# Down-projection weights fetched as whole tiles, row stores and reloads lagged, and weight preparation respaced in an adaLN transformer block on Trainium2

## The chip, the core and the metric

The kernel runs on one core of a Trainium2 chip, in one launch. A core has a matrix engine (TensorE, "PE" in the profile, with its weight loads shown apart as "PEld"), a vector engine (VectorE, "DVE"), a scalar engine (ScalarE, "ACT"), a general engine (GpSimd, "POOL"), and a sync engine (SyncE, "SP"), which in this kernel does one thing: it issues every DMA, in the order in which it is given them. The metric is the device time of one execution in microseconds (us), lower is better.

## The reference

One transformer block with conditioning, S = 2048 rows of D = 512:

```python
mod = (silu(c) @ w_mod)                    # six rows of 512: sa, ca, ga, sb, cb, gb
h = layernorm(x) * (1 + ca) + sa
q = h @ wq                                 # 32 heads of 128
k, v = last 512 rows of the cache          # 8 kv heads, each for 4 q heads
x = x + ga * (softmax(q k^T * 128**-0.5) v) @ wo
h = layernorm(x) * (1 + cb) + sb
x = x + gb * (gelu(h @ w_gate) * (h @ w_up)) @ w_down      # width 1792
```

## The kernel before

**Arithmetic.** Every operand of a large product is held as a pair of fp16 tiles, high and low part, and every product of two such pairs is three matmuls: high by high, high by low, low by high (`mm3`, lines 85, 86 and 87). Projections and the feed-forward part save products by a seven-product scheme for 2x2 blocks: sums and differences of the weight blocks are formed once, stored in DRAM (`KEPT`, tile name kept) and fetched again as "sets" of tiles w, w0 to w2 and x3.

**Attention** is 512 slots, numbered t (T = 512); a slot is 128 rows of one head against 512 keys. PE makes the scores of slot t in one of two PSUM banks named ps (`scores`). DVE takes their maximum (nm, L939). ACT takes the exponential (ee, L948), which frees the bank for slot t+2. Two slots later ACT writes the high part of the probabilities (p, L962), one slot after that DVE writes the low part (L967), and SP transposes them by DMA (pt, L971) for the product with v (po). Rows of wo (py), the query projections (qa, qb, qc) and the accumulation into acc (L888) lie between. In attention the order on every engine is written out by hand: each piece of side work is put at a slot.

**Weight preparation.** The feed-forward weights must be scaled, split and stored before the feed-forward part. That is side work of slots 286 to 511, in seven rounds of 30 slots, n = 0 to 6: gate set `prep_set(2n)`, up set `prep_set(2n+1)`, and two blocks of w_down (`prep_wd`). A `prep_set` that begins at slot b loads two tiles rw (2 buffers, so each load needs a buffer that POOL has finished with), has ACT take the sum of squares of each (`sumsq`, writes junk, L216) at slots b+1 and b+2, gets its scale fsc from DVE (L293) at b+7, and has POOL scale, combine and split them (L160, L1360, L156, L157) from b+7 to b+12. The rw buffers come free at b+11 and b+12. A load is put at the slot three ahead of its use, or one after its buffer comes free if that is later, though never after the slot of its use:

```python
        go = pos[0] - ahead
        free = released[kind].pop(0) + LDGAP
        pending[kind].append((max(min(max(go, free), pos[0]), 0), max(free + 3, pos[0] - 9), load))
```

**Feed-forward part.** 28 rows q of seven products each. The first pass (q below 14) does the first half of the rows of x and multiplies its results with w_down as it goes (`y_tasks`, whole tiles wo). The second pass (q from 14) does the other half, and its down-projection is a list of products: `down` for pairs of hidden blocks in three groups, 14 products for each, then eight of `down_last`. Each `down` product fetches what it needs of w_down just before: two halves of 128 KB of two stored tiles (`fetch_w`, called by `prefetch` four to six products ahead). At the change of passes the eight finished row tiles acc are stored to the output (`f_final`), and the same buffers take the partial rows y of the other half (`load_facc`), up to two reloads pending until row q = 16. In the feed-forward part only SP's queue has its order written by hand.

Of the kernel before, what the change touches and what calls it, by code (L numbers as in the profile page):

```python
# [17 lines left out]
P = 128  # L18
# [44 lines left out]
def block_kernel(ctx: ExitStack, tc: tile.TileContext, x, kT, v, wq, wo, wg, wu, wd, cT, wc, wm, out):  # L63
# [192 lines left out]
    def w_spread(pr, m, w=None):  # L256
        w, u, t, r = w or w_first(m), little("lu", 1, 2), little("lt", 1, 2), little("lr", 1, 2)
        pool_ts(u, w, col("kmax", pr // 2), col("ma"))
        nc.gpsimd.tensor_tensor(t, u, half_, op=ALU.pow)
        pool_ts(t, t, TOP15, 1.0, ALU.min)  # L260

        def inv():
            nc.vector.reciprocal(r, t)

        def last():
            pool_ts(col("qsc", pr), t, 2.0 ** -26)
            pool_ts(r, r, u)
            pool_ts(col("ksc", pr), r, col("kinv", pr // 2))

        if now[0] >= 0:  # L270
            then(lambda: (nc.vector.reciprocal(col("wsc", pr), w), inv(), last()), 3 if pr > 1 else 2)
        return inv, last

    def y_scale(qd):
        pool_ts(col("ysc", qd), col("ysc", qd), col("vmax", qd), 1.0 / TOP15)
# [748 lines left out]
    def begin():  # L1024
        now[0] = -1
        for i in range(QT):
            na[i][0]()
            na[i][1]()
        na[2][2]()
        na[3][2]()  # L1030
        na[0][2]()
        na[1][2]()
        na[2][3]()
        na[3][3]()
        for key in ("B", "C", "Y", "T2", "T1"):
# [12 lines left out]
        m = {}  # L1048
        pair_stat(0, m, 0)
        pair_stat(0, m, 1)  # L1050
        k0[1]()
        ts(cols[:, 1, :], cols[:, 1, :], 1.0, None, ALU.add)
        ts(cols[:, 0, :], mps[:, 0:KT], 1.0, None, ALU.mult)
        pst = {}

        def mid():
            o0[0][0]()
            pst["w"] = sums(m["m"], 2)
            o0[1][0]()
# [12 lines left out]
        for n in range(1, KT):  # L1072
            o0[n][1](False)
            o0[n][3]()
            if n == 1:
                o0[0][2](nc.gpsimd)
            if n == 2:
                inv_k()
                inv_t()
                last()  # L1080
        warm(4)
        low_w(0)
        o0[1][2]()
        o0[2][2](nc.gpsimd)
        low_k = k0[3](True)
        o0[3][2]()
        low_k()
        nb[0][0]()
        nb[0][1]()
        high_w(1)  # L1090
        q_first(warm)
        v0[1]()
        run(("d", 0))
        low_w(1)
# [297 lines left out]
    def prep_wd(n, b):  # L1392
        m, st = {}, {}
        outs = [staged() for _ in range(4)]
        l, r = slice(0, 256), slice(256, 512)

        def load(k):
            st[k] = raw("raw")
            dma(st[k], wd[(2 * n + k) * P:(2 * n + k + 1) * P, :])

        def stat(k):
            if not m:
                m["m"] = little("lm", 4, dtype=BF16)
            sumsq(m["m"][:, k:k + 1], st[k])

        def spread():
            d_spread(n, m["m"])

        def scaled(k):
            nc.gpsimd.tensor_tensor(st[k], st[k], rows[5], op=ALU.mult)  # L1410
            times(st[k], col("dsc", n))

        def minus(o, a, b):
            nc.gpsimd.tensor_tensor(st[o[0]][:, o[1]], st[a[0]][:, a[1]], st[b[0]][:, b[1]], op=ALU.subtract)

# [24 lines left out]
        if n < NP - 1:  # L1440
            sched(b + 11, (more, [s2, nop]), b + 13)
            sched(b + 12, (outs[2][1], [lambda: halves(outs[2][0]["t"], st[2]), keep_it(2)]), b + 15)
            sched(b + 13, (outs[3][1], [lambda: halves(outs[3][0]["t"], st[0]), keep_it(3)]), b + 16)

    at(T // 2 + 34, lambda: mod_row(5))
    for n in range(NP):
        b = T // 2 + 30 + 30 * n
        prep_set(2 * n, b)
        prep_set(2 * n + 1, b + 14)
        prep_wd(n, b + 23)  # L1450
    for k in range(2):
        at(T - 1 + 2 * k, lambda k=k: WO.update({("f", 0, k): fetch(("wd", 0, k), get_wo())}))
    for q, ps_ in ((0, (T - 18, T - 17, T - 16, T - 15)), (1, (T - 8, T - 7, T - 3, T)), (2, (T + 2, T + 3, T + 4, T + 5))):
# [135 lines left out]
                post()  # L1589
                run(("d", now[0] + 1))  # L1590

    load_later, ready, queue = [], [], []
    facc, done_to = {}, [0]
    SPOT = {1: (1, 0), 2: (0, 0), 3: (0, 1), 4: (3, 0), 5: (2, 0), 6: (2, 1), 7: (3, 1)}
    INTO = {1: (1, 0), 2: (1, 0), 6: (1, 1), 7: (0, 1), 4: (0, 0), 5: (0, 1), 3: (1, 1)}
    YORDER = (1, 2, 6, 7, 4, 5, 3)
# [12 lines left out]
    FACC = [(1, 0, 0), (1, 0, 1), (0, 0, 1), (0, 0, 0), (1, 1, 0), (1, 1, 1), (0, 1, 1), (0, 1, 0)]  # L1609

    def f_final(ti):
        dma(rows_of(out, ti), acc[ti])
        load_later.append(FACC.pop(0))

    def down(ns, u, k, st):
        box = {}

        def fetch_w():
            box["w"] = get_wo().rearrange("p a (n c) -> p n a c", n=2)
            j, side = SPOT[k]  # L1620
            for i, n in enumerate(ns):
                dma(box["w"][:, i], KEPT["wd", n % NP, j][:, :, side * 256:side * 256 + 256])

        def go():
            key = "a" if k in (1, 6, 7, 4) else "b" if k == 2 else "c"
# [2 lines left out]
            for r in range(2):  # L1628
                ps = st[key][:, r * 256:r * 256 + 256]
                sl = slice((2 * u + r) * P, (2 * u + r + 1) * P)  # L1630
                for i, n in enumerate(ns):
                    t, w = A[n][k], box["w"][:, i]
                    mm3(ps, t[:, 0, sl], t[:, 1, sl], w[:, 0, :], w[:, 1, :], r + i == 0 and k in (1, 2, 5), r == 1 and i == len(ns) - 1 and k in (2, 4, 3), True)
            q, h = INTO[k]
            flat = facc[q, u, h].rearrange("p r c -> p (r c)")
            by = col("dmx", ns[0] % NP // 2)
            nc.vector.scalar_tensor_tensor(flat, st[key], by, flat, op0=ALU.mult, op1=ALU.add)

        return fetch_w, go

    plain = {}

    def down_last(u, q, h, first):
        n = 2 * NP - 1

        def fetch_w():
            if first:
                for j in range(2):
                    plain[j] = fetch(("wd", n % NP, j), get_wo())

        def go():
            ps = bank("acc", "yl", NACC)
            for r in range(2):
                sl = slice((2 * u + r) * P, (2 * u + r + 1) * P)
                for j in range(2):
                    t, w = A[n][(("11", "21"), ("12", "22"))[q][j]], plain[j][:, :, h * 256:h * 256 + 256]
                    mm3(ps[:, r * 256:r * 256 + 256], t[:, 0, sl], t[:, 1, sl], w[:, 0, :], w[:, 1, :], r + j == 0, r + j == 2, True)
            flat = facc[q, u, h].rearrange("p r c -> p (r c)")
            nc.vector.scalar_tensor_tensor(flat, ps, col("dysc", n % NP), flat, op0=ALU.mult, op1=ALU.add)
            store_facc(q, u, h)  # L1660

        return fetch_w, go

    for i in range(NP, 2 * NP - 1, 2):
        for u in range(2):
            st = {}
            queue += [(i + 1,) + down((i, i + 1), u, k, st) for k in YORDER]
    queue += [(2 * NP - 1,) + down_last(u, q, h, not (u or q or h)) for q in range(2) for u in range(2) for h in range(2)]

    def prefetch(ahead=6):  # L1670
        while done_to[0] < min(len(queue), len(ready) + ahead):
            queue[done_to[0]][1]()
            done_to[0] += 1

    def down_next():
        queue[len(ready)][2]()
        ready.append(1)

    def y_step(q, k):
# [3 lines left out]
                down_next()  # L1683
        elif nexty and k in ((1, 2, 5, 6) if q < 2 * NP else (2, 5)):
            all_of(nexty.pop(0))
        if q > 2 * NP + 1:
            prefetch(4 if q < 2 * NP + 4 else 6)

    def load_next(q):
        if len(load_later) > 2 or load_later and q > 2 * NP + 1:  # L1690
            load_facc(*load_later.pop(0))

    ORDER = (1, 2, 6, 7, 5, 4, 3)

# [3 lines left out]
    for n in range(1, NP):  # L1698
        for k in range(2):
            f_at(2 * n + 1, 2 * k, lambda n=n, k=k: WO.update({("f", n, k): fetch(("wd", n, k), get_wo())}))  # L1700
    for q in range(3, NQ):
        for k, at_ in ((0, 2), (3, 2), (1, 3), (2, 4)):
            f_at(q - 1, at_, lambda q=q, k=k: set_fetch(("f", q), ("f", q % (2 * NP)), k))
# [20 lines left out]
    for q in range(NQ):  # L1724
        n, m = divmod(q, 2)
        its = items(NG + q) if q < 2 else f_items(q)
        for k, pk in enumerate(ORDER):
# [3 lines left out]
                all_of(its[pk])  # L1731
            run(("f", q, k))
            y_step(q, k)
            load_next(q)
        if m == 1 and n < NP:
            for qi, (a, b) in enumerate((("11", "21"), ("12", "22"))):
                for i in range(QT):
# [2 lines left out]
    while len(ready) < len(queue):  # L1740
        prod[0] += 1
        run(("z", prod[0]))
        prefetch()
        down_next()
    for d in range(6):
        run(("z", prod[0] + d))
# [35 lines left out]
```

## Time and profile before

| | |
|---|---|
| runs | 1743.59, 1742.16, 1743.31 us (median 1743.31) |
| profiled execution | 1743.97 us, span of its trace 1742.2 us |
| granted PE clock, mean | 0.999 of full speed |
| PE busy | 1711.4 us, 98% of the span, 8266 matmuls |
| DVE, ACT, POOL busy | 85%, 70%, 60% |
| DMA | 341.30 MB, mean 196 GB/s |

The trace starts at 0 us; preparation and the first projections take the first some 90 us, attention lasts until about 1320 us, the feed-forward part until the end, its second pass about the last 200 us. In a row of the trace stand the start and the length in us, engine, line, operation, output<-input, the count, and in brackets the time the engine stood idle before the row and what released it.

### The profile page before, as it was taken

The page shows a single profiled execution, that of the slowest core. Times are in us where ns is not written, and L with a number is a line of the kernel's source. Part 1 is how long each engine was busy: PE and PEld are TensorE (multiplying, and loading weights), DVE is VectorE, ACT ScalarE, POOL GpSimd, SP SyncE. Part 2 cuts the span into 40 slices and gives each one's busy share as a digit, 9 for nine tenths or more (in the row PEclk, how much of TensorE's full clock was granted, in tenths as well). Part 3 has the DMA queues.
Part 4 walks back from the last instruction along what each step waited for, and adds up shares of the span by engine and source line. Part 5 has one row for each costly group of instructions (what it writes and reads, how often), then busy time and mean ns, then how long its engine had stood idle before and what let it go on. Part 6 is the DMA issues. An engine that isn't in the chain of part 4 may idle for free.

```text
span 1742.2 us, 26556 instructions
## 1 busy us (share of the span) xinstructions
PE 1711.4 (98%) x8266; PEld 809.9 (46%) x8266; DVE 1477.6 (85%) x2535; ACT 1219.4 (70%) x2731; POOL 1040.1 (60%) x1242
## 2 busy tenths in 40 slices
PE   7999999999999999999999999999999999999998
PEld 4344444444444444444444444444444444444566
DVE  7888898989998898998898898899885788767676
ACT  6988888888888777688777787778773344444442
POOL 4889768787787844656577768577633323122440
PEclk9999999999999999999999999999999999999999
DMA  6989999999999988999999999999996545354453
GB/s 211 233 191 215 208 230 210 237 207 232 223 205 238 226 197 166 198 209 215 233 213 202 231 224 214 232 211 236 219 211 159 168 115 140 97 157 149 127 154 95
DMA packets 717742, 341.30 MB, mean 196 GB/s; under 512 B 598432, under 2 KB 634528, under 8 KB 717600
## 3 DMA queue, kind: packets, MB, share of 16 engines
q1 hardware_dynamic: 717312, 339.08, 85.6%
q8 instruction: 65, 1.06, 0.3%
q14 instruction: 77, 0.63, 0.1%
q10 hardware_dynamic: 288, 0.52, 0.1%
HBM read 137.50 MB, written 56.75 MB: 111 GB/s over the span
## 4 chain that ended last, share of the span: by engine, by line
PE 88%; POOL 3%; DVE 2%; DMA 2%; ACT 2%; issue 2%; SPq 1%; POOLq 0%; ACTq 0%
PE py L85 7%; PE py L86 7%; PE py L87 7%; PE po L85 6%; PE po L87 6%; PE po L86 6%; PE ps L85 6%; PE ps L86 6%; PE ps L87 6%; PE qa L85 3%; PE qa L87 3%; PE qa L86 3%; PE fa L85 3%; PE fa L87 3%; PE fa L86 3%
## 5 line engine op out<-in xcount | busy, mean ns | idle before, releaser
L948 ACT ACTIVATE ee<-ps,nm 128x512 f32<-128x512 f32 x512 | 350.6, 685 | 241.6 <-DVE nm L939 238.4
L967 DVE SCALAR_TENSOR_TENSOR p<-ee,rr,p 128x512 f16<-128x512 f32 x512 | 463.3, 905 | 2.7 <-ACT p L962 2.3
L939 DVE TENSOR_REDUCE nm<-ps 128x1 f32<-128x512 f32 x512 | 350.8, 685 | 117.5 <-PE ps L87 113.7
L962 ACT ACTIVATE p<-ee,rr 128x512 f16<-128x512 f32 x512 | 362.9, 709 | 7.8 <-DMA pt<-p 7.3
L85 PE MATMUL po<-pt,v 128*128 128x512 f16 x512 | 194.0, 379 | 7.2 <-DMA pt<-p 5.3
L85 PE MATMUL ps<-k,qt 128*128 128x512 f16 x512 | 193.9, 379 | 3.4 <-ACT ee L948 2.3
L87 PE MATMUL ps<-k,qt 128*128 128x512 f16 x512 | 194.0, 379 | 0.3 <-DVE qt L678 0.3
L87 PE MATMUL po<-pt,v 128*128 128x512 f16 x512 | 194.0, 379 | 0.0
L86 PE MATMUL py<-wo,ot 128*128 128x512 f16 x512 | 194.0, 379 | 0.0
L87 PE MATMUL py<-wo,ot 128*128 128x512 f16 x512 | 194.0, 379 | 0.0
L86 PE MATMUL po<-pt,v 128*128 128x512 f16 x512 | 194.0, 379 | 0.0
L85 PE MATMUL py<-wo,ot 128*128 128x512 f16 x512 | 194.0, 379 | 0.0
L86 PE MATMUL ps<-k,qt 128*128 128x512 f16 x512 | 193.9, 379 | 0.0
L1239 POOL TENSOR_TENSOR fg<-fg 128x512 f32<-128x512 f32 x24 | 35.6, 1482 | 137.5 <-DVE fg L1301 123.8
L85 PEld LDWEIGHTS <-w 128*128 128x128 f16 x728 | 71.2, 98 | 90.3 <-DMA w<-kept 7.9
L87 PEld LDWEIGHTS <-w 128*128 128x128 f16 x728 | 71.3, 98 | 86.1 <-issue 0.6
L86 PEld LDWEIGHTS <-w 128*128 128x128 f16 x728 | 71.3, 98 | 83.5 <-issue 1.5
L948 ACT ACTIVATION_READ_ACCUMULATOR ee<-ps,nm 128x1 f32 x512 | 99.2, 194 | 0.0
L496 POOL TENSOR_TENSOR turn<-xs,turn 128x512 f16<-128x512 f32 (+1 forms) x48 | 56.8, 1185 | 66.7 <-ACT turn L493 66.6
L888 DVE SCALAR_TENSOR_TENSOR acc<-py,ysc,acc 128x512 f32<-128x512 f32 x112 | 82.9, 740 | 10.9 <-PE py L87 10.9
L678 DVE SCALAR_TENSOR_TENSOR ot<-po,ot 128x512 f16<-128x512 f32 x128 | 86.2, 673 | 5.1 <-ACT ot L677 4.5
L85 PEld LDWEIGHTS <-v 128*128 128x128 f16 x524 | 51.2, 98 | 71.2 <-issue 10.5
(316 smaller groups left out, 4038.1 us busy)
## 6 DMA issues: line engine op xcount, KB each, us to landing
w<-kept SPq DMA_DIRECT2D x123, 256.0 KB, 3.3
kept<-stage SPq DMA_DIRECT2D x68, 256.0 KB, 3.0
raw<-in_wo SPq DMA_DIRECT2D x56, 256.0 KB, 3.3
wo<-kept SPq DMA_DIRECT2D x48, 256.0 KB, 3.5
wo<-kept SPq DMA_DIRECT2D x84, 128.0 KB, 3.1
kept<-w SPq DMA_DIRECT2D x39, 256.0 KB, 3.3
rw<-in_wq SPq DMA_DIRECT2D x38, 256.0 KB, 3.2
pt<-p SPq DMA_TRANSPOSE x512, 3.5
```

Of the source, the lines that this page charges most:

```text
L85: nc.tensor.matmul(ps, lhi, rhi, start=first, stop=False, skip_group_check=chain)
L86: nc.tensor.matmul(ps, lhi, rlo, start=False, stop=False, skip_group_check=chain)
L87: nc.tensor.matmul(ps, llo, rhi, start=False, stop=last, skip_group_check=chain)
L496: nc.gpsimd.tensor_tensor(S[s][:, :, 1, :], side(s), S[s][:, :, 0, :], op=ALU.subtract)
L678: return lambda: nc.vector.scalar_tensor_tensor(t[:, 1, :], src, scale, t[:, 0, :], op0=ALU.mult, op1=ALU.subtract)
L888: nc.vector.scalar_tensor_tensor(acc[ti], st["p"], by, acc[ti], op0=ALU.mult, op1=ALU.add)
L939: nc.vector.tensor_reduce(nm, E[t]["ps"], axis=AX.X, op=ALU.max, negate=True)
L948: nc.scalar.activation(e, E[t]["ps"], AF.Exp, bias=E[t]["nm"], scale=1.0, accum_out=sm[:, t % 2:t % 2 + 1])
L962: nc.scalar.activation(p16[:, 0, :], E[t]["e"], AF.Copy, scale=E[t]["r"])
L967: nc.vector.scalar_tensor_tensor(p16[:, 1, :], E[t]["e"], E[t]["r"], p16[:, 0, :], op0=ALU.mult, op1=ALU.subtract)
L1239: nc.gpsimd.tensor_tensor(o, a, b, op=op)
```

## The change

Three parts.

1. **Second pass.** Each of the 26 stored w_down tiles that the second pass uses is fetched once, whole (256 KB, `tile_fetch`), at a row and product written in a table (`FETCH`), and `down` slices it. One tile in four goes to another buffer (name wl). The stores of `f_final` are put two products later than the step that asks for them, and each reload six products later, so that a reload stands four products behind its store; `prefetch` and `load_next` go.
2. **Weight preparation.** In each round of 30 slots the up set begins at b+10 (was b+14) and w_down at b+18 (was b+23). In `prep_wd` the scaling of a block by the row gb and by its scale is one DVE instruction instead of two of POOL.
3. **Beginning.** The four low parts of the first activations (L446) are all written by DVE (two were POOL's), after the first weights' low part; the scale ksc is made by DVE in one step, where POOL took two; these small steps follow the four high parts.

```diff
 # w_spread: first call only
+        def last_dve():
+            pool_ts(col("qsc", pr), t, 2.0 ** -26)
+            ts(col("ksc", pr), r, u, col("kinv", pr // 2))
-        return inv, last
+        return inv, last if now[0] >= 0 else last_dve
 # beginning
             o0[n][3]()
-            if n == 1:
-                o0[0][2](nc.gpsimd)
-            if n == 2:
-                inv_k()
-                inv_t()
-                last()
+        inv_k()
+        inv_t()
+        last()
         warm(4)
         low_w(0)
-        o0[1][2]()
-        o0[2][2](nc.gpsimd)
         low_k = k0[3](True)
-        o0[3][2]()
+        for n in range(KT):
+            o0[n][2]()
 # prep_wd
         def scaled(k):
-            nc.gpsimd.tensor_tensor(st[k], st[k], rows[5], op=ALU.mult)
-            times(st[k], col("dsc", n))
+            nc.vector.scalar_tensor_tensor(st[k], st[k], col("dsc", n), rows[5], op0=ALU.mult, op1=ALU.mult)
 # weight preparation
         prep_set(2 * n, b)
-        prep_set(2 * n + 1, b + 14)
-        prep_wd(n, b + 23)
+        prep_set(2 * n + 1, b + 10)
+        prep_wd(n, b + 18)
 # second pass
     def f_final(ti):
-        dma(rows_of(out, ti), acc[ti])
-        load_later.append(FACC.pop(0))
+        lag(2, lambda: dma(rows_of(out, ti), acc[ti]))
+        lag(6, lambda: load_facc(*FACC.pop(0)))
+    def tile_fetch(n, j):
+        t = pool.tile([P, 2, 512], F16, tag="ln", name="wl", bufs=3) if j == 1 else get_wo()
+        TILE[n, j] = fetch(("wd", n % NP, j), t)
 # down
-        def fetch_w():
-            box["w"] = get_wo().rearrange("p a (n c) -> p n a c", n=2)
-            j, side = SPOT[k]
-            for i, n in enumerate(ns):
-                dma(box["w"][:, i], KEPT["wd", n % NP, j][:, :, side * 256:side * 256 + 256])
-                    t, w = A[n][k], box["w"][:, i]
+                    t, w = A[n][k], TILE[n, j][:, :, cols_]
 # y_step
-        if q > 2 * NP + 1:
-            prefetch(4 if q < 2 * NP + 4 else 6)
+    FETCH = (((15, 5), (15, 6), (16, 0), (16, 1), (16, 5), (16, 6), (17, 0), (17, 1)),
...
+    for g, spots in enumerate(FETCH):
+        for p, spot in enumerate(spots):
+            f_at(*spot, lambda n=NP + 2 * g + p % 2, j=(1, 0, 2, 3)[p // 2]: tile_fetch(n, j))
```

How the instructions move, at three places. A row names the line, the operation, output<-input with the number of each tile, and the semaphores waited for. Lines from L939 on stand four higher in the changed kernel.

First, SP's queue in the round n = 1, around the slot in which ACT uses the first rw tile of the up set; before:

```order
L93 DMA kept_10943<-stage_10748 128x1024 [waits DMAHW7_49,Pool_49]
L971 DMA_TRANSPOSE pt_10953<-p16_10925 128x8x128 [waits DMAHW0_49,DVE_49,PE_49]
L93 DMA x3_10974<-kept_2662 128x512 [waits DMAHW1_49]
L971 DMA_TRANSPOSE pt_10953<-p16_10959 128x8x128 [waits DMAHW2_49,DVE_49,Activation_49]
L93 DMA rw_11001<-in_wu 128x512 [waits DMAHW3_49,Pool_49]
```

and after:

```order
L93 DMA kept_10945<-stage_10698 128x1024 [waits DMAHW1_49,Pool_49]
L975 DMA_TRANSPOSE pt_10955<-p16_10927 128x8x128 [waits DMAHW2_49,DVE_49,PE_49]
L93 DMA rw_10974<-in_wu 128x512 [waits DMAHW3_49,Pool_49]
L975 DMA_TRANSPOSE pt_10955<-p16_10961 128x8x128 [waits DMAHW4_49,DVE_49,Activation_49]
L93 DMA rw_11005<-in_wu 128x512 [waits DMAHW5_49,Pool_49]
```

The load of rw stands one transpose, which is one slot, earlier.

Second, ACT's queue at the same place; before, from the slot of p16_10925 and p16_10959 (the two transposes above) to the use of that tile:

```order
L948 ACTIVATE ee_10955,sm_10923<-ps_10945,nm_10949 128x512 [waits DVE_49]
L952 ACTIVATE rr_10957<-sm_10923 128x2 [waits Activation_49]
L962 ACTIVATE p16_10959<-ee_10888,rr_10890 128x512 [waits DMAHW2_49]
...
L948 ACTIVATE ee_11079,sm_11048<-ps_11068,nm_11072 128x512 [waits DVE_49]
L952 ACTIVATE rr_11081<-sm_11048 128x2 [waits Activation_49]
L962 ACTIVATE p16_11083<-ee_11016,rr_11018 128x512 [waits DMAHW2_49]
L677 ACTIVATE ot_11094<-po_11060 128x512 [waits PE_49]
L216 ACTIVATE junk_90,lm_11098<-rw_11001 128x512 [waits DMAHW3_49]
```

and after:

```order
L952 ACTIVATE ee_10957,sm_10925<-ps_10947,nm_10951 128x512 [waits DVE_49]
L956 ACTIVATE rr_10959<-sm_10925 128x2 [waits Activation_49]
L966 ACTIVATE p16_10961<-ee_10890,rr_10892 128x512 [waits DMAHW4_49]
L681 ACTIVATE ot_10972<-po_10938 128x512 [waits PE_49]
L216 ACTIVATE junk_90,lm_10978<-rw_10974 128x512 [waits DMAHW3_49]
L952 ACTIVATE ee_10990,sm_10991<-ps_10980,nm_10984 128x512 [waits DVE_49]
```

The use of the tile moved four slots up (four rows ee), and now stands in the slot of p16_10961, whose transpose SP issues behind the load; the next row ee stands behind the use.

Third, SP's queue in the second pass, where the last row tiles acc are stored and partial rows reloaded; before:

```order
L93 DMA out_y<-acc_17309 128x512 [waits DVE_49]
L93 DMA acc_19109<-y5_17101 128x2x256 [waits DMAHW7_49,DMAHW6_49]
L93 DMA wo_19148<-kept_10906 128x2x256 [waits DMAHW0_49]
L93 DMA wo_19148<-kept_11883 128x2x256 [waits DMAHW1_49]
L93 DMA wo_19151<-kept_10876 128x2x256
L93 DMA wo_19151<-kept_11858 128x2x256 [waits DMAHW3_49]
L93 DMA wo_19154<-kept_10718 128x2x256 [waits DMAHW4_49]
L93 DMA wo_19154<-kept_11687 128x2x256 [waits DMAHW5_49]
L93 DMA w0_19184<-kept_12353 128x1024
```

and after:

```order
L93 DMA acc_19063<-y7_17181 128x2x256 [waits DMAHW3_49,DMAHW2_49]
L93 DMA out_y<-acc_17254 128x512 [waits DVE_49]
L93 DMA w2_19077<-kept_12084 128x1024 [waits DMAHW4_49]
L93 DMA out_y<-acc_17294 128x512 [waits DMAHW5_49,DVE_49]
L93 DMA acc_19133<-y5_17086 128x2x256 [waits DMAHW6_49,DMAHW3_49]
L93 DMA w0_19162<-kept_12239 128x1024 [waits DMAHW7_49]
```

The six half fetches and the reload directly behind its own store are gone from ahead of the weight fetch w0.

More of the change, by code (lines that the diff above doesn't have):

```diff
@@ L1590, in all_of @@
                 run(("d", now[0] + 1))
-    load_later, ready, queue = [], [], []
-    facc, done_to = {}, [0]
+    ready, queue = [], []
+    facc = {}
     SPOT = {1: (1, 0), 2: (0, 0), 3: (0, 1), 4: (3, 0), 5: (2, 0), 6: (2, 1), 7: (3, 1)}
@@ L1611, in f_final @@
     def f_final(ti):
-        dma(rows_of(out, ti), acc[ti])
-        load_later.append(FACC.pop(0))
-    def down(ns, u, k, st):
-        box = {}
-        def fetch_w():
-            box["w"] = get_wo().rearrange("p a (n c) -> p n a c", n=2)
-            j, side = SPOT[k]
-            for i, n in enumerate(ns):
-                dma(box["w"][:, i], KEPT["wd", n % NP, j][:, :, side * 256:side * 256 + 256])
+        lag(2, lambda: dma(rows_of(out, ti), acc[ti]))
+        lag(6, lambda: load_facc(*FACC.pop(0)))
+    TILE = {}
+    def tile_fetch(n, j):
+        t = pool.tile([P, 2, 512], F16, tag="ln", name="wl", bufs=3) if j == 1 else get_wo()
+        TILE[n, j] = fetch(("wd", n % NP, j), t)
+    def down(ns, u, k, st):
+        j, side = SPOT[k]
+        cols_ = slice(side * 256, side * 256 + 256)
         def go():
@@ L1637, in go, with down_last @@
             nc.vector.scalar_tensor_tensor(flat, st[key], by, flat, op0=ALU.mult, op1=ALU.add)
-        return fetch_w, go
-    plain = {}
-    def down_last(u, q, h, first):
+        return go
+    def down_last(u, q, h):
         n = 2 * NP - 1
[L1646 to L1649, printed above, removed]
         def go():
@@ L1655, in go @@
                 for j in range(2):
-                    t, w = A[n][(("11", "21"), ("12", "22"))[q][j]], plain[j][:, :, h * 256:h * 256 + 256]
+                    t, w = A[n][(("11", "21"), ("12", "22"))[q][j]], TILE[n, j][:, :, h * 256:h * 256 + 256]
                     mm3(ps[:, r * 256:r * 256 + 256], t[:, 0, sl], t[:, 1, sl], w[:, 0, :], w[:, 1, :], r + j == 0, r + j == 2, True)
@@ L1660, in go @@
             store_facc(q, u, h)
-        return fetch_w, go
+        return go
     for i in range(NP, 2 * NP - 1, 2):
@@ L1666, in block_kernel @@
             st = {}
[L1667 to L1673, printed above, removed]
+            queue += [(i + 1, down((i, i + 1), u, k, st)) for k in YORDER]
+    queue += [(2 * NP - 1, down_last(u, q, h)) for q in range(2) for u in range(2) for h in range(2)]
     def down_next():
-        queue[len(ready)][2]()
+        queue[len(ready)][1]()
         ready.append(1)
@@ L1685, in y_step @@
             all_of(nexty.pop(0))
-        if q > 2 * NP + 1:
-            prefetch(4 if q < 2 * NP + 4 else 6)
-    def load_next(q):
-        if len(load_later) > 2 or load_later and q > 2 * NP + 1:
-            load_facc(*load_later.pop(0))
     ORDER = (1, 2, 6, 7, 5, 4, 3)
@@ L1700, in block_kernel @@
             f_at(2 * n + 1, 2 * k, lambda n=n, k=k: WO.update({("f", n, k): fetch(("wd", n, k), get_wo())}))
+    FETCH = (((15, 5), (15, 6), (16, 0), (16, 1), (16, 5), (16, 6), (17, 0), (17, 1)),
+             ((20, 5), (20, 6), (21, 0), (21, 1), (22, 0), (22, 0), (22, 1), (22, 1)),
+             ((24, 5), (24, 6), (25, 0), (25, 1), (26, 0), (26, 0), (26, 1), (26, 1)))
+    for g, spots in enumerate(FETCH):
+        for p, spot in enumerate(spots):
+            f_at(*spot, lambda n=NP + 2 * g + p % 2, j=(1, 0, 2, 3)[p // 2]: tile_fetch(n, j))
+    for j in range(2):
+        f_at(26, 6 - j, lambda j=j: tile_fetch(2 * NP - 1, j))
     for q in range(3, NQ):
@@ L1733, in block_kernel @@
             y_step(q, k)
-            load_next(q)
         if m == 1 and n < NP:
@@ L1742, in block_kernel @@
         run(("z", prod[0]))
-        prefetch()
         down_next()
```

## The prediction

> **What bounds the kernel now.** I read the page first, for the share of each engine and the chain.
>
> ```profile
> PE 1711.4 (98%) x8266; PEld 809.9 (46%) x8266; DVE 1477.6 (85%) x2535; ACT 1219.4 (70%) x2731; POOL 1040.1 (60%) x1242
> ```
> ```profile
> PE 88%; POOL 3%; DVE 2%; DMA 2%; ACT 2%; issue 2%; SPq 1%; POOLq 0%; ACTq 0%
> ```
> ```profile
> rw<-in_wu SPq DMA_DIRECT2D x14, 256.0 KB, 3.2
> ```
>
> PE is busy 1711.4 of 1742.2 us, so at most 30.8 us can be won, and the change takes no matmul away. Whatever it does to the time it does by adding or removing idle time of PE, or by its clock. So the next view is the list of PE's waits (what it waited for, us in total, times, longest):
>
> ```profile
> PE po L85 <- DMA pt<-p: 5.3, 6, 3.2
> ...
> PE fa L85 <- DMA w<-kept: 4.1, 1, 4.1
> PE ps L85 <- ACT ee L948: 2.3, 3, 1.3
> PE po L85 <- issue: 1.9, 1, 1.9
> PE fb L85 <- DMA w<-kept: 1.5, 1, 1.5
> ...
> PE fc L85 <- DVE acc L888: 0.8, 1, 0.8
> ...
> PE pq L1019 <- POOL B L446: 0.4, 1, 0.4
> ```
>
> fa, fb and fc are feed-forward banks, waits of the second pass; pq is the beginning; ps and po are attention. In the stretches where weight preparation lies, PE has no idle time, as the table of windows shows (length, then busy us of PE, PEld, DVE, ACT, POOL):
>
> ```profile
> 1000.00:1100.00 100.00, 100.00 (x468) 45.39 (x467) 88.37 (x153) 80.38 (x189) 67.41 (x86) 1.00 1.06 227
> ```
>
> So there the change has nothing to win, only to lose. DVE has 11.6 us spare per 100, ACT 19.6.
>
> **The second pass.** The timeline of SP and of PE at its largest wait:
>
> ```profile
> 1575.09 0.43 SPq L93 DMA_DIRECT2D out_y<-acc  x1
> 1579.35 0.37 SPq L93 DMA_DIRECT2D acc<-y  x1
> 1579.76 4.50 SPq L93 DMA_DIRECT2D wo<-kept  x6
> 1584.31 0.60 SPq L93 DMA_DIRECT2D w<-kept  x1
> ```
> ```profile
> 1587.68 0.39 PE L85 MATMUL fa<-B,w 128*128 128x512 f16 x1 [4.12 <-DMA w<-kept]
> ```
>
> SP stands from 1575.52 to 1579.35, 3.8 us, since the reload writes the buffer that the store ahead of it reads; then six half fetches take 4.50 us of issue; w0 comes after both and lands 3.4 us later, 4.12 late. In the changed order a reload is four products behind its store (a product is at least six matmuls, at 100 / 468 = 0.214 us by the window above: 4 x 6 x 0.214 = 5.1 us or more, against 3.8), and no half fetch stands between store and w0. So the 4.12 goes. With it goes time at half clock (the windows' seventh value after the length is the granted clock):
>
> ```profile
> 1588.00:1589.00 1.00, 1.00 (x6) 0.40 (x5) 0.46 (x1) 0.00 (x0) 1.00 (x1) 0.93 0.91 269
> 1589.00:1590.00 1.00, 1.00 (x4) 0.34 (x3) 0.00 (x0) 0.65 (x2) 0.47 (x1) 0.50 0.99 308
> ```
> ```profile
> 1592.00:1593.00 1.00, 1.00 (x10) 0.82 (x9) 0.96 (x2) 0.00 (x0) 0.00 (x0) 0.87 0.00 0
> ```
>
> Lost there: 0.07 + 3 x 0.50 + 0.13 = 1.7 us (the two rows between also have 0.50). The shorter wait of 3.20 us at the start of attention has no such stretch behind it:
>
> ```profile
> 95.15 0.38 PE L85 MATMUL po<-pt,v 128*128 128x512 f16 x1 [3.20 <-DMA pt<-p]
> ```
> ```profile
> 96.00:98.00 2.00, 2.00 (x11) 0.93 (x10) 0.71 (x3) 0.85 (x2) 1.27 (x2) 1.00 1.02 236
> ```
>
> The 1.5 (fb) has the same build of store, reload and fetch, and the 0.8 (fc) is PE waiting for the accumulation that precedes a store. All of it is 4.12 + 1.7 + 1.47 + 0.79 = 8.1 us. What is late next: three fetches of sets (w0_19041, w2_19077, w0_19162) remain behind a store that waits for DVE, with 0 to 2.5 us in hand when I lay SP's new order on the old times. That may cost 0 to 2.4; I take 0.8, nearer nothing, as the issue time ahead of them shrinks. Gain 7.3, between 5.7 and 8.1. The 26 whole fetches move what 52 of the 84 halves' count would; their issue on SP, some 0.4 us each by the rows of out_y and acc above, lies beside PE's matmuls with nothing that PE needs soon behind it, and costs nothing; where a weight fetch is close behind, it costs what the 0.8 allows.
>
> **The weight preparation.** ACT must read each rw tile for its sum of squares, and in its fixed order the exponential of the slot stands behind that. Before, the load stands in SP's queue one slot after the buffer is free and ACT uses it three slots on. Now the up set's use falls into the slot in which the buffer is freed, so the load is put into the same slot: ACT cannot have the data in time. The trace has one such wait already, with a load that was late:
>
> ```profile
> 935.81 1.16 POOL L157 TENSOR_TENSOR stage<-rw,stage 128x512 f16<-128x512 f32 x1
> ```
> ```profile
> 936.99 0.34 SPq L93 DMA_DIRECT2D rw<-in_wu  x1
> ```
> ```profile
> 939.50 0.63 ACT L216 ACTIVATE junk<-rw 128x512 f16<-128x512 f32 x1 [1.21 <-DMA rw<-in_wu]
> ```
>
> POOL ends its last read of the buffer at 936.97, SP issues at 936.99, and the data is there 2.51 later. The page's median landing is 3.2. Now the round n = 1, on DVE, POOL, SP, ACT and PE:
>
> ```profile
> 839.33 0.15 DVE L293 RECIPROCAL fsc<-lw 128x1 f32<-128x1 f32 x1
> ```
> ```profile
> 842.86 1.13 POOL L160 TENSOR_SCALAR rw<-rw,fsc 128x512 f32<-128x512 f32 x1
> ```
> ```profile
> 853.39 1.16 POOL L157 TENSOR_TENSOR stage<-rw,stage 128x512 f16<-128x512 f32 x1
> ```
> ```profile
> 854.57 0.34 SPq L93 DMA_DIRECT2D rw<-in_wu  x1
> ```
> ```profile
> 860.88 0.62 ACT L216 ACTIVATE junk<-rw 128x512 f16<-128x512 f32 x1
> ```
> ```profile
> 861.50 0.67 ACT L948 ACTIVATE ee<-ps,nm 128x512 f32<-128x512 f32 x1
> ```
> ```profile
> 865.07 0.38 PE L85 MATMUL ps<-k,qt 128*128 128x512 f16 x1
> ```
>
> From 842.86 to 854.55 POOL works 11.7 us on the gate set. It begins late here, since w_down's splitting of the round before comes first; five slots earlier that is out of the way, and the set begins with its scale, at about 839.9. The buffer is then free at 851.6, SP issues at about 852.0, and the data is there at 855.2. A slot is (1240.92 - 860.88) / 150 = 2.53 us (the row of 1240.92 is the same step five rounds later, below). ACT comes to the use four slots earlier, at 860.88 - 10.1 = 850.8, and waits 4.4. Behind it stands ee, which frees the bank of the scores two slots on: ee ends at 862.17 and PE needs the bank at 865.07, 2.9 in hand, so PE would wait 4.4 - 2.9 = 1.5. In round 6:
>
> ```profile
> 1234.47 0.51 SPq L93 DMA_DIRECT2D rw<-in_wu  x1
> ```
> ```profile
> 1240.92 0.62 ACT L216 ACTIVATE junk<-rw 128x512 f16<-128x512 f32 x1
> ```
> ```profile
> 1241.54 0.67 ACT L948 ACTIVATE ee<-ps,nm 128x512 f32<-128x512 f32 x1
> ```
> ```profile
> 1243.72 0.38 PE L85 MATMUL ps<-k,qt 128*128 128x512 f16 x1
> ```
>
> with the load 2.6 us earlier, at 1231.9, data at 1235.1, ACT there at 1230.8: a wait of 4.3, and 1243.72 - 1242.21 = 1.5 in hand, so PE waits 2.8. The other five rounds, laid out in the same way, give ACT waits of 4.4 to 6.5 and PE waits of 1.5 to 3.8. I take 2.3 for each of seven: 16 us. The bounds: with a landing of 2.51 instead of 3.2 each is 0.7 to 0.8 less, some 10.5; with all at the largest, 3.8, it is 26. The transposes behind p come late too, but po has about 5.6 us in hand there, so they add nothing to what the scores already wait; without that margin, up to the difference of 1 us a round. The second tile's load and use both stand a slot later, so its wait is shared with the first.
>
> Moving the scaling from POOL to DVE:
>
> ```profile
> L475 DVE SCALAR_TENSOR_TENSOR xs<-xs,rs,row 128x512 f32<-128x512 f32 x24 | 21.5, 895 | 0.0
> ```
> ```profile
> L160 POOL TENSOR_SCALAR raw<-raw,dsc 128x512 f32<-128x512 f32 x14 | 13.6, 968 | 5.4 <-DVE dsc L307 4.2
> ```
>
> The new form is not there; the nearest row has the same shape and operands and takes 0.9. Two in a round of 76 us are 1.8 us of DVE, against 8.8 spare (11.6 per 100): cost nothing, hidden by that spare; without it 14 x 0.9 = 12.6. POOL gains over 0.97 a block, which is not on PE's path. The single waits of attention (1.9 for issue, and of the 2.3 the part that falls into the preparation, 0.5) lie where preparation work crowds a slot: I let 0.5 of them go.
>
> **The beginning.** PE waited 0.4 for POOL's low part; DVE, which does the other two lows at 0.64, takes that over. Gain 0.4, between 0 and 0.6; it cannot cost much, since DVE's extra two steps, 1.3 us, are covered by the first low parts' matmuls; if they are not, it is a loss of 0.9.
>
> **Sum.** 1743.97 + 16 - 0.5 - 0.4 - 7.3 = 1751.8 against the profiled execution. That one is 0.66 above the median of the three runs shown, so against the median 1751.1; I say 1751.
>
> [...]
>
> **Rivals.** One, on the other side: the two score banks and ACT's spare time hide the new waits. For it: the 1.21 us at 939.50 is not in PE's list with a matching wait of ps. Against it: the waits worked out are three to five times that, above the 1.5 to 2.9 in hand. If PE waits 0 to 0.5 a round, 0 to 3.5 in all, the time is 1751.1 - 16 + (0 to 3.5) = 1735 to 1739. It decides when the seven together stay below 8.2 - 3.5 = 4.7 us, 0.7 a round. Two: the waits are longer than the path by POOL gives, because SP itself is late at its transposes, and some exceed what let the clock stand (between 3.20 and 4.12 us). Then 3 to 3.5 us of waiting in each of seven, 23, and two or three drops at 1.7 give 1743.3 + 23 + 4 - 8 = 1762. Three: the second pass keeps its waits, since the whole tiles are now late or stores still hold SP ahead of w0: 7.3 comes down to 3, and the time is 1755. Four, between: 0.7 to 1.7 us a round, 5 to 12 in all, which pays back the 8.2 won: 1740 to 1747.
>
> **How the numbers follow.** My forecast 0.44, rival one 0.21, two 0.13, three 0.08, four 0.14. A change of 0.2%, 3.5 us, is about what a measurement of this kernel can tell from none. Faster by more is below 1739.8, rival one: 0.21. Slower by more is above 1746.8: forecast, two and three, 0.65. The rest, 0.14, is rival four. The forecast's own range goes by its bounds, 10.5 to 26 less 5.7 to 8.6, 1745 to 1763. To hold 8 in 10 the range must take in most of rival one, so it runs from 1736 to 1763.
>
> **What would show it.** In the trace after, ACT's junk rows of the up sets (seven) should stand behind 3 to 6 us of idle time put down to the rw load, and PE's list should have some seven waits of ps for ee, 10 to 26 us together; SP should show rw directly after POOL's L157. In the second pass fa, fb and fc should have left the list, with clock 1.00 throughout. The forecast is wrong if ps has no such waits, if the load goes out much before POOL's splitting (a buffer free earlier than I think), or if DVE's new steps push nm, which would show as ps waits for ee with ACT waiting for nm.

## The result and the profile after

The changed kernel takes 1759.36 us (median of four runs, 1758.56 to 1760.40) against 1743.45 us before (1742.16 to 1745.67): a ratio of 1.009 with an interval of 1.0073 to 1.0108, 15.9 us slower. A second measurement gave 1759.00, ratio 1.0099 [1.0085, 1.0113]. The forecast of 1751 had the sign right and the size at half.

The page of the changed kernel, the engines' busy time and the chain of work that ended last:

```profile
PE 1715.1 (98%) x8264; PEld 810.2 (46%) x8266; DVE 1485.1 (85%) x2552; ACT 1218.3 (69%) x2731; POOL 1001.9 (57%) x1210
...
PE 80%; DVE 9%; DMA 3%; ACT 3%; POOL 3%; issue 2%; SPq 1%; POOLq 0%; ACTq 0%; DVEq 0%
```

The span is 1756.8 us. PE's idle time grew from 30.8 to 41.7 us, and PE's busy time grew too, by 3.7 us, for the same matmuls: 3.4 of that is clock, as the stretches below show. The list of PE's waits after the change begins with

```profile
PE ps L85 <- ACT ee L952: 21.1, 11, 4.4
PE sps L126 <- DVE mv L391: 4.8, 1, 4.8
PE po L85 <- DMA pt<-p: 3.1, 4, 1.6
```

and the waits of fb and fc, and of fa for w, are gone. The table of windows says in which stage the time went; first the kernel before, then the changed one (the stretch, its length, then busy us of PE, PEld, DVE, ACT, POOL, the granted clock, DMA share, GB/s):

```profile
700.00:1300.00 600.00, 597.57 (x2788) 270.91 (x2786) 532.63 (x909) 468.30 (x1097) 394.67 (x473) 1.00 1.01 218
1300.00:1500.00 200.00, 199.31 (x925) 90.24 (x923) 153.94 (x243) 87.50 (x152) 61.14 (x56) 1.00 0.54 142
1500.00:1700.00 200.00, 193.59 (x1068) 104.41 (x1067) 142.32 (x201) 92.57 (x149) 65.28 (x47) 0.99 0.48 142
1700.00:1742.00 42.00, 37.36 (x290) 28.09 (x287) 26.27 (x39) 8.90 (x15) 1.59 (x2) 1.00 0.30 94
```
```profile
700.00:1300.00 600.00, 579.88 (x2679) 261.12 (x2678) 517.47 (x890) 450.39 (x1056) 359.39 (x444) 0.99 0.97 209
1300.00:1500.00 200.00, 199.31 (x924) 90.15 (x923) 153.39 (x247) 93.49 (x171) 53.66 (x50) 1.00 0.61 157
1500.00:1700.00 200.00, 200.00 (x1088) 106.22 (x1087) 152.73 (x214) 96.38 (x155) 64.10 (x47) 1.00 0.41 126
1700.00:1756.00 56.00, 50.44 (x371) 35.97 (x368) 37.87 (x53) 15.14 (x25) 11.12 (x8) 0.98 0.23 74
```

In the 600 us in which weights are prepared PE got through 109 matmuls fewer (2788 to 2679, some 23 us of work); between 1500 and 1700 us it has no idle time left (193.59 to 200.00). Most of the loss is the wait that was forecast. Here is round n = 1 of the changed kernel, on SP, POOL, ACT and PE:

```profile
853.28 1.23 SPq L975 DMA_TRANSPOSE pt<-p  x1
854.60 0.53 SPq L93 DMA_DIRECT2D rw<-in_wu  x1
```
```profile
852.76 1.47 POOL L157 TENSOR_TENSOR stage<-rw,stage 128x512 f16<-128x512 f32 x1
```
```profile
857.50 0.63 ACT L216 ACTIVATE junk<-rw 128x512 f16<-128x512 f32 x1 [3.77 <-DMA rw<-in_wu]
858.13 0.67 ACT L952 ACTIVATE ee<-ps,nm 128x512 f32<-128x512 f32 x1
```
```profile
858.94 0.38 PE L85 MATMUL ps<-k,qt 128*128 128x512 f16 x1 [0.95 <-ACT ee L952]
```

SP issues the load at 854.60, the data is there 2.90 us later, and ACT has stood 3.77 us for it. Then ee follows, and PE, which needs the bank that ee frees, has stood 0.95. The seven rounds have ACT waits of 5.12, 3.77, 5.16, 5.88, 3.92, 4.47 and 4.97 and PE waits of 3.48, 0.95, 3.21, 4.36, 2.49, 2.46 and 1.67, and one of 0.63 behind the sixth: 19.3 us of PE waits. In rounds 0, 2 and 3 the clock fell as well; round 2, PE and the clock (the value ahead of the DMA share, 0.82, then 0.50):

```profile
938.28 0.59 PE L85 MATMUL ps<-k,qt 128*128 128x512 f16 x1 [3.21 <-ACT ee L952]
```
```profile
937.00:938.00 1.00, 0.00 (x0) 0.00 (x0) 0.00 (x0) 1.00 (x3) 0.00 (x0) 0.82 1.09 354
938.00:939.00 1.00, 0.72 (x2) 0.26 (x2) 0.13 (x1) 1.00 (x4) 0.00 (x0) 0.50 0.17 48
939.00:940.00 1.00, 1.00 (x4) 0.37 (x3) 0.87 (x2) 1.00 (x4) 0.00 (x0) 0.50 0.00 0
940.00:941.00 1.00, 1.00 (x4) 0.39 (x3) 0.57 (x2) 0.97 (x4) 0.00 (x0) 0.50 0.08 15
```

PE has half its clock from 937.64 to 941.04, 3.4 us, and loses 1.7 by the clock alone. Three of these are 5.1 us; the one of before, at 1588.86, is gone, which leaves 3.4 more than before.

### The profile page after: what moved, and what is told of

Read it like the earlier page. It is cut to its first block, busy times and chain, and to the rows that moved or that the text cites. A ratio compares the mean times of both kernels' runs of the same rounds, so it can differ in the third digit from the quotient of the medians.

```text
span 1756.8 us, 26455 instructions
## 1 busy us (share of the span) xinstructions
PE 1715.1 (98%) x8264; PEld 810.2 (46%) x8266; DVE 1485.1 (85%) x2552; ACT 1218.3 (69%) x2731; POOL 1001.9 (57%) x1210
## 4 chain that ended last, share of the span: by engine, by line
PE 80%; DVE 9%; DMA 3%; ACT 3%; POOL 3%; issue 2%; SPq 1%; POOLq 0%; ACTq 0%; DVEq 0%
PE py L87 6%; PE py L86 6%; PE py L85 6%; PE ps L85 5%; PE ps L87 5%; PE ps L86 5%; PE po L87 5%; PE po L85 5%; PE po L86 5%; PE fa L85 3%; PE fa L87 3%; PE fa L86 3%; PE qa L85 2%; PE qa L87 2%; DVE p L971 2%; PE qa L86 2%
## 5 line engine op out<-in xcount | busy, mean ns | idle before, releaser
L971 DVE SCALAR_TENSOR_TENSOR p<-ee,rr,p 128x512 f16<-128x512 f32 x512 | 457.5, 894 | 21.0 <-ACT p L966 20.6
L85 PE MATMUL ps<-k,qt 128*128 128x512 f16 x512 | 194.4, 380 | 22.1 <-ACT ee L952 21.1
L233 POOL TENSOR_TENSOR lw<-lw,half__86 128x1 f32<-128x1 f32 x37 | 21.8, 589 | 135.4 <-DVE lw L183 135.4
L500 POOL TENSOR_TENSOR turn<-xs,turn 128x512 f16<-128x512 f32 (+1 forms) x48 | 56.8, 1184 | 63.1 <-ACT turn L497 62.9
```

Of the source, the lines that this page charges most:

```text
L85: nc.tensor.matmul(ps, lhi, rhi, start=first, stop=False, skip_group_check=chain)
L233: nc.gpsimd.tensor_tensor(out, out, half_, op=ALU.pow)
L500: nc.gpsimd.tensor_tensor(S[s][:, :, 1, :], side(s), S[s][:, :, 0, :], op=ALU.subtract)
L971: nc.vector.scalar_tensor_tensor(p16[:, 1, :], E[t]["e"], E[t]["r"], p16[:, 0, :], op0=ALU.mult, op1=ALU.subtract)
```

## The experiments

Theory A: the rw load of the up set is issued in the slot in which ACT uses it; ACT stands for it ahead of ee, PE for ee, and the longer waits lower the clock. Theory B: the offsets only show where; the DVE steps or the whole tiles crowd attention. All times stand beside runs of the kernel before on the same chip.

**Offsets back, the rest as changed.**

```diff
-        prep_set(2 * n + 1, b + 10)
-        prep_wd(n, b + 18)
+        prep_set(2 * n + 1, b + 14)
+        prep_wd(n, b + 23)
```

> The changed kernel with the up set and w_down put back to b+14 and b+23; the DVE scaling, the beginning and the second pass stay as changed. Theory A (the same-slot rw loads make ACT wait, ACT's wait keeps the score banks, and the longest of these waits also cost clock): the trace after has 18.6 us of seven ps waits plus 0.6 behind them, and three stretches of half clock of 3.4 us, 1.7 lost each, so 1759.4 - 19.2 - 5.1 = 1735, with no ps wait over 1.5 us in attention after 100 us. Theory B (DVE's 14 new steps or the whole tiles crowd attention, and the offsets only show where): the waits stay in some form and the time is 1750 or more.

Measured: 1736.73 us (1735.69 to 1738.20), ratio 0.9967 [0.9957, 0.9978]. Of ps waits for ee its list has three, 2.8 us in all; two of them, at 44 and 62 us, lie ahead of the preparation, and the one within it is 0.31. Theory B falls: DVE's steps and the whole tiles are in this kernel.

**Offsets alone.** The kernel before with b+10 and b+18.

> The kernel before with only the two offsets changed to b+10 and b+18. Theory A: seven ACT waits for rw of 4 to 6 us, some 19 us of ps waits and two to four clock drops: 1743.4 + 19 + 5 = 1767 (1763 to 1771), slower than the changed kernel since the second pass gives nothing back. Theory B: 1743 to 1747.

Measured: 1766.89 us (1764.26 to 1769.90), ratio 1.0139 [1.0121, 1.0156], 24 us slower by nothing but two numbers. Its waits:

```profile
PE ps L85 <- ACT ee L948: 19.8, 12, 4.3
...
PE fa L85 <- DMA w<-kept: 4.3, 1, 4.3
```

**Second pass alone.**

> The kernel before with only the second pass changed (whole tiles, lagged stores and reloads). By the prediction's sum 8.1 us go (waits 4.12, 1.47, 0.79, and 1.7 of clock) less 0 to 2.4 of new ones: 1735.3 to 1738. The rival that the whole tiles are late or that stores still hold SP: 1740 or more, with fa or fb waits for w in the list.

Measured: 1735.54 us (1734.27 to 1736.05), ratio 0.9958 [0.9945, 0.9972], between 4.9 and 9.6 us faster by that interval. No wait of fa, fb or fc for w or acc is in its list. The forecast gain of 7.3 lies inside that. How much of it the lagged stores and reloads bring and how much the whole tiles was not tried apart.

**The up set at b+12 in place of b+10.**

> The changed kernel with the up set at b+12 in place of b+10 (w_down stays at b+18). The rw load is then put into slot b+12 and ACT uses it at b+13, one slot of 2.53 us between. Theory A: each ACT wait of 3.8 to 5.9 us shrinks by about 2.5, PE's by as much, to under 1 us or nothing, and no wait costs clock: 1735 to 1738. Rival: it is POOL's crowding in the round (sets and w_down closer together) that delays the buffer, so the waits move along: 1750 or more.

Measured: 1738.30 us (1736.20 to 1741.45), ratio 0.9974 [0.9964, 0.9984]. ACT still waits 0.7 to 2.8 us for the first tile, and no PE wait in the preparation reaches 0.6. Two slots more gave back 21 of the 23 us that the offsets cost (1759.36 less 1736.73).

**The up set at b+11.** Here the load goes to slot b+12, the use too.

> The changed kernel with the up set at b+11. By the rule of the load's slot (one after the release, never after the use) the rw load goes to slot b+12 and ACT uses it in b+12 too: the same slot again, but POOL has had one slot more. Theory A1, that the load's place in SP's queue behind that slot's transposes sets the wait: ACT waits of 3 to 4.5 us remain, PE waits some 8 us in all, with no or one clock drop: 1743 to 1747. Theory A2, that POOL's release of the buffer alone sets it: waits shorter by a whole slot, under 3 us, PE under 2 us in all: 1736 to 1739.

Measured: 1755.77 us (1753.55 to 1761.34), ratio 1.0082 [1.0069, 1.0095]. POOL had one slot more, and it did not help. SP, POOL and ACT in round n = 1:

```profile
855.82 1.23 SPq L975 DMA_TRANSPOSE pt<-p  x1
857.14 0.57 SPq L93 DMA_DIRECT2D rw<-in_wu  x1
```
```profile
852.27 1.56 POOL L157 TENSOR_TENSOR stage<-rw,stage 128x512 f16<-128x512 f32 x1
```
```profile
860.44 0.63 ACT L216 ACTIVATE junk<-rw 128x512 f16<-128x512 f32 x1 [5.50 <-DMA rw<-in_wu]
```

The buffer was free at 853.83, and the load went out at 857.14, behind the transposes of its slot, which themselves follow ACT's p and DVE's low part of that slot. ACT came to the use at 854.94, before SP had even got to the load. Of its wait of 5.50, 2.20 are this late issue and 3.30 the load itself, so a load in the slot of its use came late though POOL had long been done. In all seven rounds the load goes out 0.1 us behind a transpose, 0.5 to 3.8 after POOL's read. The ps waits are 17.1 us, 1.9 to 2.5 in six of the rounds, and this time no clock fell in the preparation. Both amounts I gave for A1 were too low (8 us of waits, 1743 to 1747): with A1 right, the waits are nearly as long as at b+10 (21.1).

**One slot earlier in SP's queue, offset unchanged.**

```diff
-        free = released[kind].pop(0) + LDGAP
+        free = released[kind].pop(0) + (0 if kind == "rw" and pos[0] > T // 2 + 30 else LDGAP)
```

> The up set at b+11 as in the run before, but the rule of the load's slot for rw in the preparation is the slot of the release itself, not one after: the load moves one slot up in SP's queue, ahead of one transpose, and is still behind POOL's last read of the buffer. There the trace of b+11 has POOL's read ending at 853.83 (round n = 1) and SP issuing only at 857.14, behind the transposes. If the place in the queue sets the wait (A1), the load goes out 2.5 to 3.3 us earlier, ACT waits 2 to 3 us, PE under 0.5 a round: 1737 to 1741. If POOL's release, or the set's time in the round, sets it (A2): unchanged, 1754 to 1757.

Measured: 1742.60 us (1739.84 to 1743.92), ratio 1.0001 [0.9992, 1.0010]: 13 us less than b+11, by the place of one kind of load in a queue. In the two profiled executions 10.3 of it is PE's idle time between 700 and 1300 us (18.3 and 8.0); 1.7 is a stretch of half clock at 93.29 us, ahead of the preparation, which only the execution of b+11 has. The same round:

```profile
850.78 0.53 SPq L93 DMA_DIRECT2D rw<-in_wu  x1
```
```profile
848.94 1.47 POOL L157 TENSOR_TENSOR stage<-rw,stage 128x512 f16<-128x512 f32 x1
```
```profile
854.00 0.63 ACT L216 ACTIVATE junk<-rw 128x512 f16<-128x512 f32 x1 [2.22 <-DMA rw<-in_wu]
```

The load goes out 0.37 after POOL's read ends, ACT waits 1.7 to 4.0 us, PE 1.0 to 2.1 in four of the rounds. That is 1.6 us above what I expected, since in four rounds the PE wait did not fall under 0.5.

**Extra work in the waits.** Matmuls of a constant into a bank that nobody reads:

```diff
+EXTRA = {300: 12, 360: 11, 390: 16, 420: 8, 450: 8, 480: 4}
...
+            if t in EXTRA:
+                eb = bank("acc", "extra", NACC)
+                for _ in range(EXTRA[t]):
+                    nc.tensor.matmul(eb, ones.to_broadcast([P, P]), ones.to_broadcast([P, 512]), start=True, stop=True)
             if t < T:
                 scores(t)
```

> The changed kernel with extra matmuls of a constant by a constant into a bank that nobody reads, put just ahead of the scores that wait for ee: 12, 0, 11, 16, 8, 8 and 4 in the seven rounds, each about as many as fit into the wait that the trace of the changed kernel shows there (59 in all, 12.6 us of PE at 0.214). If the three stretches of half clock come from PE standing idle, they go and the 59 matmuls cost nothing: 1759.4 - 5.1 = 1754. If the clock falls for another reason (load, or what the waiting engines do), or if idle time alone makes the loss, 1759 or up to 1761.

Measured: 1755.82 us (1754.13 to 1757.00), ratio 1.0078 [1.0066, 1.0090]. The time is nearer to the first case, but its interval overlaps with 1.009 [1.0073, 1.0108], from another measurement. So both kernels were run once more, side by side:

> The changed kernel once more, on the same chip as the run with extra matmuls beside it: 1757 to 1761, with two to five stretches of half clock in the preparation, at other rounds perhaps, since they begin only at the edges of a grid of 3.413 us that does not follow the program.

> The kernel with 59 extra matmuls once more, beside the changed kernel on one chip. If idle PE lowers the clock: 2 to 5 us faster than the changed kernel in spite of the extra work, with no half clock in the preparation. If not: equal or slower by up to 2.

Measured: changed kernel 1759.00 us (1758.11 to 1760.97), with the extra matmuls 1754.29 us (1753.78 to 1755.23). 59 matmuls more make the kernel 4.7 us faster. The page, the list of waits and the windows of the changed kernel, then the same three of the one with extra work (an added line shifts its numbers by one):

```profile
PE 1715.1 (98%) x8266; PEld 811.1 (46%) x8266; DVE 1486.7 (85%) x2552; ACT 1218.8 (69%) x2731; POOL 1000.9 (57%) x1210
```
```profile
PE ps L85 <- ACT ee L952: 21.6, 12, 4.4
```
```profile
700.00:1300.00 600.00, 580.05 (x2676) 261.39 (x2674) 517.04 (x890) 450.23 (x1056) 359.32 (x444) 0.99 0.98 209
```
```profile
PE 1722.7 (98%) x8325; PEld 815.1 (46%) x8325; DVE 1482.5 (85%) x2552; ACT 1217.9 (69%) x2731; POOL 1003.4 (57%) x1210
```
```profile
PE ps L86 <- ACT ee L953: 9.3, 10, 1.3
```
```profile
700.00:1300.00 600.00, 591.90 (x2754) 267.72 (x2752) 517.40 (x894) 451.98 (x1061) 361.36 (x444) 1.00 0.98 211
```

The ps waits shrink by 12.3, the extra matmuls fill 59 x 0.214 = 12.6 of them, so the waiting itself is what it was; PE's busy time grew by 7.6 and not by 12.6, and the difference of 5.0 is the three stretches of half clock, which are gone (1.00 in the window).

**The scaling alone, the beginning alone.**

> The kernel before with only the scaling of w_down as one DVE instruction in place of two of POOL. By the prediction 14 x 0.9 us of DVE are hidden: within 1 us of before. Rival: without cover, up to 12.6 us more, shown by ps waits for ee with ACT waiting for nm, or po waits for pt.

> The kernel before with only the beginning changed. By the prediction 0.4 us less, between 0.9 more and 0.6 less; the pq wait for POOL's low part is gone from the list.

Measured: 1742.31 us, ratio 1.0007 [0.9998, 1.0016], and 1742.30 us, ratio 1.0001 [0.9992, 1.0010]. Neither can be told from nothing. With the scaling alone the 14 DVE steps take 0.74 us each (0.9 was the estimate):

```profile
L1410 DVE SCALAR_TENSOR_TENSOR raw<-raw,dsc,gate 128x512 f32<-128x512 f32 x14 | 10.4, 744 | 0.0
```

and no ps wait came of them. Whether the beginning's 0.4 is there is open, since it lies inside the interval; with the beginning alone, PE's wait for POOL is gone from the list.

**Second pass and beginning, preparation as before.**

> The kernel before with the new second pass and the new beginning, and the weight preparation left as it was (offsets and POOL scaling). A candidate for faster than both: 1735 to 1737 by the runs of the parts, 7 less than before and 23 less than the changed kernel; above 1740 if the parts do not add.

Measured: 1734.36 us (1733.84 to 1734.82), ratio 0.9956 [0.9943, 0.9968]: 8 us faster than before and 25 faster than the changed kernel. It is the fastest of all that ran, though not apart from the second pass alone (1735.54). One late fetch stands in its list, a wait of fa for w of 0.4.

```profile
PE 1709.2 (99%) x8266; PEld 809.8 (47%) x8266; DVE 1482.4 (86%) x2538; ACT 1219.0 (70%) x2731; POOL 1034.2 (60%) x1238
```

## Why the prediction was half right

By the steps of its sum, against the profiled executions (1743.97 to 1758.56, +14.6):

| term | forecast | in the traces |
|---|---|---|
| PE waits of the seven rounds | +16 (10.5 to 26) | +19.3 |
| clock in these waits | 0, left to rival two | +5.1, three stretches |
| single waits of attention | -0.5 | -1.9 (1.87 and 0.47 gone, 0.43 new) |
| beginning | -0.4 | -0.8, all waits up to 40 us; alone not measurable |
| second pass | -7.3 | -6.4 of waits and -1.7 of clock, +1.5 at the end |
| not in the sum | 0 | -0.9, waits between 40 and 130 us |
| sum | +7.8 | +14.2 |

The mechanism was right in every link: the load in the slot of its use, ACT's wait ahead of ee, the score bank, the second pass won. The offsets alone and the offsets undone show it from both sides, and the parts come near to the whole (24 up, 7 down, 16 measured).

**The term that failed is the clock.** The prediction saw the price (1.7 us a stretch) and its own estimate had waits of up to 3.8 us, yet it put no clock into the likeliest sum. It read from two rows, 3.20 without a drop and 4.12 with one, that a wait has to be longer than something between these. That step is wrong. The waits behind which the clock fell were 3.48, 3.21 and 4.36 us in the changed kernel, and with the offsets alone it fell after 2.29 and 2.55 too, PE and clock:

```profile
1101.08 0.54 PE L85 MATMUL ps<-k,qt 128*128 128x512 f16 x1 [2.29 <-ACT ee L948]
```
```profile
1101.00:1102.00 1.00, 0.92 (x3) 0.40 (x3) 0.32 (x1) 0.64 (x2) 0.00 (x0) 0.58 0.89 275
1102.00:1103.00 1.00, 1.00 (x4) 0.30 (x2) 0.92 (x2) 0.44 (x1) 0.00 (x0) 0.50 0.32 94
```

The last section has what was measured: 2.08 us of idle time in one cell of a grid were enough. With 5.1 in the sum the forecast would have been +12.9, against +14.6. That it is three stretches is partly the luck of the grid: waits of 2.49 and 2.46 us kept the full clock here, while with the offsets alone it fell in four of the seven rounds, once for twice as long.

**The waits were mis-sized by a fifth** (2.3 a round, measured 2.75). The prediction timed the load by POOL's release of the buffer. In the changed kernel that let the load go in rounds 0, 2, 3 and 5, 0.36 us after POOL's read in round 0 and 0.03 after it in the others. In rounds 4 and 6 POOL was done 0.9 and 1.1 us earlier, and the load went out 0.1 behind SP's transpose, a condition that the prediction had only in rival two and that the run at b+11 shows alone. In round 1 both fell together (POOL's read ends at 854.23, SP's transpose at 854.51, the load goes out at 854.60). The estimate for round 1 (ACT 4.4, PE 1.5; measured 3.77 and 0.95) and for round 6 (4.3 and 2.8; 4.97 and 1.67) was right within 1.2 us; rounds 0, 2 and 3 are above the mean. ACT's waits, 3.77 to 5.88, are no longer than the 4.3 to 6.5 of the prediction, so the fifth hardly comes from a later load; less time in hand between ACT's wait and PE's would account for it, but this stays open, since the prediction gives five of them only as a range.

**The second pass came out as forecast.** The reload no longer stands on its store, w is in time, and all three waits are gone, as is the half clock at 1588.86. The 0.8 kept for late fetches was not spent there; instead the end after PE's last matmul grew, from 4.8 to 6.4 us, by PE's idle time between 1700 us and the end of the span in the windows above (42.2 - 37.36 and 56.8 - 50.44). The last six stores begin 1.0 us before PE's last matmul ends, where it was 2.2 before; why was not tried.

**Rivals.** The first (banks and spare time hide the waits) fell: its point of decision was 0.7 us a round, and only one round of seven was near that. It describes what b+12 does, though: there ACT waits up to 2.8 us and PE pays nothing worth the name. The second had the right amounts, three drops and some 3 us a round, and 1762, though its cause, SP late at its transposes, held back the load in rounds 1, 4 and 6 only. 0.13 was too little for it, since the prediction's own waits of up to 3.8 us reached between its 3.20 and 4.12. The third and fourth fell.

## What to carry to other kernels

A prefetch distance that a rule computes can collapse silently: here moving a consumer four slots up made the rule put the load into the consumer's own slot, and the wait came at once in full, at b+10 and at b+11 (21.1 and 17.1 us of ps waits), while one slot of distance took most of it away (at b+12 no PE wait there reached 0.6). When work is moved in a hand-ordered kernel, follow the load in the queue that issues it, not only the buffer's release, and ask what stands behind the waiting instruction. And a stall of TensorE is to be priced with its clock, as the kernel's own traces show it: here one stretch of half clock cost 1.7 us, beside PE waits of 3.21 to 4.36 us ahead of it.

## What the runs showed of the hardware

In these traces the clock fell at the edges of a grid of 3.413 us. From the windows the start of each stretch of half clock can be read to about 0.01 us (0.82 in the window of 937 is full speed until 937.64). In the changed kernel the stretches begin at 780.62, 937.64 and 1019.56: 157.02 and 81.92 apart, which is 46.0 and 24.0 times 3.413 us. With the offsets alone they begin at 94.24, 783.72, 940.74, 1019.24, 1101.16 and 1613.16, which are 689.48, 157.02, 78.50, 81.92 and 512.00 apart, or 202, 46, 23, 24 and 150 times 3.413 us: all on one grid to 0.02. I laid this grid over the gaps of PE after 40 us, up to its last matmul, in fourteen traces and took PE's idle time within each cell that begins at full clock, as far as it is 0.9 us or more:

```
                                     idle in the cell      clock after it
18 cells, nine traces                2.08 to 3.41 us       half, 3.4 us or longer
77 cells, fourteen traces            0.92 to 1.96 us       full
```

So what parts the two rows in these traces is neither the length of a wait nor the sum of waits, but the idle time within one cell: at most 1.96 us in the one, at least 2.08 in the other. The 3.20 us wait of the kernel before was cut by an edge into 1.87 and 1.33, and the clock stayed at 1.00; in the kernel with only the second pass the same wait was shorter, 2.46, lay in one cell, and the clock fell:

```profile
93.52 0.38 PE L85 MATMUL po<-pt,v 128*128 128x512 f16 x1 [2.46 <-DMA pt<-p]
```
```profile
94.00:95.00 1.00, 1.00 (x5) 0.44 (x4) 0.00 (x0) 1.00 (x3) 1.00 (x2) 0.67 1.03 203
95.00:96.00 1.00, 1.00 (x4) 0.29 (x2) 0.00 (x0) 0.42 (x1) 1.00 (x2) 0.50 0.67 158
```

The edges do not follow the program: counted from the start of the trace, the grid stands at 2.38 us in one profiled execution of the changed kernel and at 0.01 in the other, with the first stretch at 780.62 and at 781.66. An estimate from the two rows, with 2.05 us (between 1.96 and 2.08) of one cell as the limit and the edge anywhere at equal chance: a single wait of 2.1 us would lower the clock in four cases of ten, one of 3.0 in two of three, and one of some 4.1 in all, since even an edge in its middle leaves 2.05 in a cell.

A second thing, seen once: with the offsets alone a wait of 4.34 us went on into the cell after the drop for 1.68 us, and the half clock lasted two cells, 1019.24 to 1026.07; where PE was idle for up to 0.69 us in the cell after the drop, the clock came back after one each time. What lies between was not tried.
